# Blocks of 512 tokens in a two-stage feed-forward kernel, and the weights' signs moved by a rectifier

## The chip, the cores and the metric

The kernel runs on one core of one Trainium2 chip. The metric is the device time of one execution in microseconds (us). A kernel is timed several times and the median is given; one execution is also recorded by the hardware profiler, and its own time stands beside its span.

## The reference

The inputs are four batches of eight heads with 576 positions of 64 numbers. Two attentions are added: a global one over means of four positions, whose output is repeated four times, and a local one over the positions less than four apart. The sum, laid out as x with 2304 tokens by 512, goes through two feed-forward stages:

```
out_up   = repeat(softmax(scale * mean4(q) @ mean4(k).T) @ mean4(v), 4)
out_loc  = softmax(where(|i-j| < 4, scale * q @ k.T, -1e9)) @ v
x  = (out_up + out_loc) as [2304, 512]
h  = x @ w_in  ;  g = where(h > 0, h, exp(min(h, 0)) - 1)  ;  x2  = g @ w_out      # stage 1, w_in [512, 2048]
h2 = x2 @ w2_in ; g2 = s * max(h2, 0)**2 + b               ;  out = g2 @ w2_out    # stage 2
```

The weights arrive as 64-bit floats. The kernel makes 32-bit numbers of them on the chip, and splits these into a high and a low part, so that three products (high by high, low by high, high by low) replace one.

## The kernel before

The tokens are cut into nine blocks of 256 (N = 256, NSUB = 9), and the 2048 inner features into 16 slices of 128 (FC = 16). Work for a stage ph, a block j and a slice f is one unit: `ffn_h` makes h (12 matmuls of 256 columns, line 879), five elementwise instructions on ScalarE, VectorE and GpSimd turn it into gh and gl (lines 899 to 915 and the helpers at 303 to 311), and `ffn_x` adds g @ w_out to two accumulators. In stage 1 these are 12 matmuls of 256 columns (line 935), in stage 2 six of 512 columns (line 938), because there w_out is the moving operand.

The order of the units is a list. Blocks 0 and 1 of stage 1 are interleaved with an offset of five slices, blocks 2 to 6 follow one by one, blocks 7 and 8 (`LASTP` = 2) alternate slice by slice, and then stage 2 takes its nine blocks one by one. A slice of weights stays in one buffer for the whole of a stage; the slice of stage 2 takes the buffer when the last block of stage 1 has used it. Blocks 7 and 8 each have an x tile from a pool of two, which also served blocks 5 and 6.

Making one weight slice (`weights`, lines 340 to 370): two DMAs of 512 KB fill `raw`; ScalarE multiplies the upper words by 2^-112, which moves the exponent (line 303, raw<-raw); VectorE shifts the lower words right by 29 (line 357), puts the sign bit of the upper word into the lower (line 362), and adds the upper word shifted left by 3 (line 364); ScalarE copies the result to w's high part (line 303, w<-raw); GpSimd or VectorE subtracts for the low part (line 311). There are 16 slices in each stage.

Nothing of this has a fixed place. A planner (`Plan.emit`) keeps a list of operations with an assumed duration, a due time and the buffers that they take, and issues on each engine the operation that can start first, earlier due times going first. The due times come from the constants at the head of the file (T0 and P0 to P2 for the units, WL for the weights, A1 to DT for the attention). Where the planner sees TensorE idle, it puts matmuls on zeros (`keep_warm`, line 1139). So the record shows TensorE busy where it only waits, and line 1139 has to be read as idle time.

Of the kernel before, what the change touches and what calls it, by code (L numbers as in the profile page):

```python
# [21 lines left out]
DIRECT = 2  # L22
# [6 lines left out]
T0, P0, LB, TR, R0, P1, P2 = 39.86, 4.909, 5, 35.22, 2.175, 2.551, 2.783  # L29
VO, N0, N1, WL, RL, A1, A2, A3, AE, XL = 1.82, -7.55, 62.49, 11.29, -35.77, 25.65, -34.57, 3.08, 64.22, 29.58  # L30
DE, DS, DT = -1.26, 98.38, 75.88
LASTP, NREST, VP = 2, 4, -1.95
# [22 lines left out]
class Plan:  # L55
# [9 lines left out]
    WAIT = 1.607  # L65
# [162 lines left out]
def attn_moe_moe2(ctx, tc, q, k, v, w_in, w_out, w2_in, w2_out, s2, b2, mask, mask_d, out):  # L228
# [59 lines left out]
    x2d = [dram_buf(f"x2d{j}", [DM, N]) for j in range(NSUB)]  # L288
# [31 lines left out]
    order += [(0, j, f) for f in range(FC) for j in range(NSUB - LASTP, NSUB)]  # L320
    order += [(1, j, f) for j in range(NSUB) for f in range(FC)]
    due_at, t = {}, T0
    for ph, j, f in order:
        due_at[ph, j, f] = t
        t += P0 if ph == 0 and j < 2 else P1 if ph == 0 else P2

    def vt(ph, j, f):
        return due_at[ph, j, f]
# [4 lines left out]
    def weights(ph, f):  # L333
# [9 lines left out]
        for i in range(2):  # L343
            def ld(i=i):
# [10 lines left out]
        copy(lambda: high().bitcast(F32), lambda: high().bitcast(F32), 2 * DM, ("act",), scale=2.0 ** -112,  # L355
             r=rawp, w=[u], u=[raw], due=due)
# [10 lines left out]
        op("dve", 0.14 + 4 * DM / 960, cv, r=[u, shifted], w=[raw], due=due, lock=True)  # L367
# [9 lines left out]

    def x_buf(ph, j):
        if (ph, j) not in x_b:
            x = Buf(*((p1, "nat") if (ph, j) == (1, 0) else (p2, "x")), [128, 2, CC, N], F32R)  # L380
            x.part = [(Buf(None, "xhi", None), Buf(None, "xlo", None)) for _ in range(CC)]
            x_b[ph, j] = x
        return x_b[ph, j]
# [353 lines left out]
    def split(xb, c, o, m, src, r, due):  # L737
        xh, xl = (list(p) for p in zip(*(xb.part[c] if isinstance(c, slice) else [xb.part[c]])))
        n = m * (c.stop - c.start if isinstance(c, slice) else 1)
        copy(lambda: xb()[:, 0, c, o:o + m], src, n, r=r, w=xh, u=[xb], due=due)  # L740
        tt(lambda: xb()[:, 1, c, o:o + m], src, lambda: xb()[:, 0, c, o:o + m].bitcast(F32), ALU.subtract, n,
           r=r + xh, w=xl, u=[xb], due=due)
# [124 lines left out]
    def ffn_h(ph, j, f, n=N):  # L867
        due = vt(ph, j, f)
        third = ph == 0 and 2 <= j < NSUB - LASTP and 3 <= f < FC - 3 and f % 3 == 0
# [6 lines left out]
        def mm(run, first, last):  # L876
            def pe():
                for i, (wpart, xpart, c) in enumerate(run):
                    nc.tensor.matmul(ps(), lhsT=w()[:, wpart, 0, c * 128:(c + 1) * 128], rhs=x()[:, xpart, c, :],  # L879
# [11 lines left out]
        for i, (run, need) in enumerate(runs):  # L891
            op("pe", us * len(run), mm(run, i == 0, i == len(runs) - 1), r=need + [ps], w=[ps], u=[w, x], due=due, ffn=True)
        e = Buf(p2, "r", [128, n])
        gh, gl = Buf(p4, "gh", [128, n], F32R), Buf(p4, "gl", [128, n], F32R)
# [3 lines left out]
        if ph == 0:  # L898
# [6 lines left out]
            copy(gh, e, n, r=[r3], w=[gh], u=[e], due=due)  # L905
            tt(gl, e, lambda: gh().bitcast(F32), ALU.subtract, n, r=[r3, gh], w=[gl], u=[e], due=due)
        else:
# [5 lines left out]
               r=[r2], w=[gh], u=[e], due=due)  # L913
            op("dve", td + 0.07, lambda: nc.vector.scalar_tensor_tensor(  # L914
                out=gl(), in0=e(), scalar=sb2[:, 1:2], in1=gh().bitcast(F32), op0=ALU.add, op1=ALU.subtract),
               r=[r2, gh], w=[gl], u=[e], due=due, lock=True)
        return gh, gl

    def ffn_x(ph, j, f, g):
        gh, gl = g  # L920
        w = w_b[ph, f]
        due = vt(ph, j, f) + 3 * (P1 if ph == 0 else P2)
        if f == 0:
            acc_b[ph, j] = [Buf(ps_a, "acc", [128, 512]) for _ in range(2)]
        for a in range(2):
            acc = acc_b[ph, j][a]

            def pe(acc=acc, a=a):
                for i, (wpart, g) in enumerate(((0, gh), (1, gh), (0, gl))):
                    wo = w()[:, wpart, 1]  # L930
                    last = f == FC - 1 and i == 2
                    if ph == 0:
                        for c in range(2):
                            cc = 2 * a + c
                            nc.tensor.matmul(acc()[:, c * N:(c + 1) * N], lhsT=wo[:, cc * 128:(cc + 1) * 128], rhs=g(),  # L935
                                             start=(f == 0 and i == 0 and c == 0), stop=last and c == 1)
                    else:
                        nc.tensor.matmul(acc(), lhsT=g()[:, a * 128:(a + 1) * 128], rhs=wo,  # L938
                                         start=(f == 0 and i == 0), stop=last)

            op("pe", 0.712, pe, r=[w.out, gh, gl, acc], w=[acc], u=[w], due=due, ffn=True)
            if f == FC - 1:
                o = Buf(p2, "ev", [128, 512])
                if ph == 0:
                    copy(o, acc, 512, r=[acc], w=[o], due=due - 4)
# [3 lines left out]
                    continue  # L949
                parts = 2 if j == NSUB - 1 else 1  # L950
                n = 512 // parts
                for i in range(parts):
                    half, c = Buf(None, "half", None), slice(i * n, (i + 1) * n)
                    copy(lambda o=o, c=c: o()[:, c], lambda acc=acc, c=c: acc()[:, c], n, ("act", "dve")[i:] if parts > 1 else ("act", "dve"),
                         r=[acc], w=[half], u=[o], due=due - 4)
                    load(Buf(None, "out", None), 262144 // parts, lambda a=a, o=o, c=c: nc.sync.dma_start(
# [247 lines left out]
```

## Time and profile before

| | us |
|---|---|
| median of three runs (lowest, highest) | 979.16 (978.72, 982.04) |
| the profiled execution: its time, its span | 976.13, 974.0 |
| TensorE busy, of the span | 955.4, 98% |
| VectorE busy | 612.4, 63% |
| ScalarE busy | 473.0, 49% |
| GpSimd busy | 409.2, 42% |
| TensorE's granted clock in the 40 slices | 0.9 or more of full speed in each |

The engines are named PE (TensorE), PEld (its weight loads), DVE (VectorE), ACT (ScalarE), POOL (GpSimd) and SP (SyncE). A duration of a single matmul in the trace is about 284 ns for 256 columns, but matmuls overlap; what one costs is read from how far apart runs of them begin. Stage 1's last two blocks begin at about 466 us, stage 2 at about 566 us.

### The profile page before, as it was taken

Reading aid. Unit: us, or ns where it says so; the run is one execution under the profiler, and the core shown is the slowest. Engines: PE = TensorE matmul, PEld = TensorE weight load, DVE = VectorE, ACT = ScalarE, POOL = GpSimd, SP = SyncE. Lnnn points to the kernel's source line nnn. Section 1 sums busy time; section 2 is a strip of 40 time slices with the busy share of each in tenths; the row PEclk is TensorE's granted clock in tenths of the full one; section 3 lists DMA queues with packets and bytes.
Section 4 is the critical chain, followed back from the end, with each engine's and each line's share of the span. In section 5 each row is a group of like instructions: output and inputs, shape, how many; then the busy total and the mean of one; then the engine's idle time right before and its main releaser. Section 6 shows DMA issues by size and latency. Waiting matters only on the chain.

```text
span 974.0 us, 21374 instructions
## 1 busy us (share of the span) xinstructions
PE 955.4 (98%) x8420; PEld 892.2 (92%) x8420; DVE 612.4 (63%) x1058; ACT 473.0 (49%) x1239; POOL 409.2 (42%) x385
## 2 busy tenths in 40 slices
PE   8999999999999999999999999999999999999998
PEld 7888898999999999999999999999999999999997
DVE  5689888897787988887367797333334343333332
ACT  6687666555554455444665565333333333333332
POOL 5565556678776887775564543010101010010000
PEclk9999999999999999999999999999999999999999
DMA  9755656553433542443333451000101010100000
GB/s 198 200 141 175 192 162 155 136 161 83 127 99 99 123 110 64 100 115 109 109 131 130 152 183 57 23 28 17 44 1 45 1 44 1 44 2 22 1 23 22
DMA packets 102468, 88.34 MB, mean 91 GB/s; under 512 B 48864, under 2 KB 91872, under 8 KB 102368
## 3 DMA queue, kind: packets, MB, share of 16 engines
q1 hardware_dynamic: 100576, 86.54, 31.7%
q8 instruction: 66, 1.08, 0.5%
q10 hardware_dynamic: 1792, 0.44, 0.2%
q14 instruction: 34, 0.28, 0.1%
HBM read 73.85 MB, written 13.11 MB: 89 GB/s over the span
## 4 chain that ended last, share of the span: by engine, by line
PE 69%; DVE 11%; POOL 6%; issue 6%; DMA 4%; ACT 3%; SPq 1%; POOLq 0%; DVEq 0%; ACTq 0%
PE h L879 31%; PE acc L938 21%; PE acc L935 12%; POOL gl L311 2%; PE acc L879 2%; DVE raw L362 2%; DMA raw<-in_moe_w_out_dram 2%; DVE raw L364 2%; POOL w L311 1%; POOL wu L311 1%; DVE raw L357 1%; DVE w L311 1%; DVE raw L822 1%; DVE r L903 1%; DMA w<-in_k_dram 1%
## 5 line engine op out<-in xcount | busy, mean ns | idle before, releaser
L879 PE MATMUL h<-x,w 128*128 128x256 f32 x3024 | 407.0, 284 | 4.0 <-DVE r L903 2.9
L879 PEld LDWEIGHTS h<-x,w 128*128 128x128 f32 x3024 | 387.0, 188 | 19.1 <-DVE r L903 5.0
L935 PE MATMUL acc<-gh,w 128*128 128x256 f32 x1152 | 188.8, 285 | 0.0
L938 PE MATMUL acc<-w,gh 128*128 128x512 f32 x576 | 181.4, 396 | 0.0
L935 PEld LDWEIGHTS acc<-gh,w 128*128 128x128 f32 x1152 | 157.3, 189 | 2.6 <-issue 1.9
L311 POOL TENSOR_TENSOR x<-xr,x 128x256 fp32r<-128x256 f32 (+2 forms) x47 | 40.9, 892 | 262.5 <-DVE x L305 254.6
L909 DVE SCALAR_TENSOR_TENSOR r<-r,sb,h 128x256 f32<-128x256 f32 x144 | 68.9, 478 | 129.2 <-ACT r L908 129.2
L311 POOL TENSOR_TENSOR gl<-r,gh 128x256 fp32r<-128x256 f32 x127 | 111.7, 884 | 81.8 <-ACT gh L303 77.0
L914 DVE SCALAR_TENSOR_TENSOR gl<-r,sb,gh 128x256 fp32r<-128x256 f32 x144 | 77.8, 541 | 101.8 <-ACT gh L912 101.8
L912 ACT ACTIVATE gh<-r,sb 128x256 fp32r<-128x256 f32 x144 | 73.2, 508 | 101.3 <-PE acc L938 86.2
L908 ACT ACTIVATE r<-h 128x256 f32<-128x256 f32 x144 | 55.0, 382 | 130.2 <-PE h L879 129.8
L935 PE MATMUL acc<-gl,w 128*128 128x256 f32 x576 | 115.6, 282 | 0.0
L938 PE MATMUL acc<-w,gl 128*128 128x512 f32 x288 | 113.5, 394 | 0.0
L938 PEld LDWEIGHTS acc<-w,gh 128*128 128x128 f32 x576 | 99.3, 188 | 13.7
L311 POOL TENSOR_TENSOR w<-raw,w 128x512 fp32r<-128x512 f32 x48 | 66.5, 1397 | 60.3 <-ACT w L303 55.8
L935 PEld LDWEIGHTS acc<-gl,w 128*128 128x128 f32 x576 | 88.6, 188 | 0.0
L903 DVE SCALAR_TENSOR_TENSOR r<-r,h 128x256 f32<-128x256 f32 x124 | 50.7, 414 | 54.3 <-ACT r L901 49.3
L303 ACT ACTIVATE gh<-r 128x256 fp32r<-128x256 f32 x144 | 58.3, 413 | 50.4 <-DVE r L903 27.6
L899 ACT ACTIVATE r<-h 128x256 f32<-128x256 f32 x124 | 46.8, 378 | 66.3 <-PE h L879 39.0
L938 PEld LDWEIGHTS acc<-w,gl 128*128 128x128 f32 x288 | 54.1, 188 | 13.5 <-DVE gl L914 0.3
L822 DVE TENSOR_REDUCE raw<-wu 128x128 f32<-128x896 f32 x36 | 63.6, 1787 | 2.0 <-POOL wu L311 1.9
L901 ACT ACTIVATE r<-r 128x256 f32<-128x256 f32 x144 | 60.0, 417 | 3.9
(144 smaller groups left out, 1170.4 us busy)
## 6 DMA issues: line engine op xcount, KB each, us to landing
raw<-in_moe_w_in_dram SPq DMA_DIRECT2D x32, 512.0 KB
raw<-in_moe_w_out_dram SPq DMA_DIRECT2D x32, 512.0 KB
raw<-in_k_dram SPq DMA_DIRECT2D x17, 320.0 KB
raw<-in_v_dram SPq DMA_DIRECT2D x17, 320.0 KB
x2d<-ev SPq DMA_DIRECT2D x18, 256.0 KB
xr<-x2d SPq DMA_DIRECT2D x18, 256.0 KB
out_dram<-ev SPq DMA_DIRECT2D x16, 256.0 KB
vg<-in_v_dram SPq DMA_DIRECT2D x12, 288.0 KB
```

The lines of the kernel that those rows point to most:

```text
L303: a = (0.11 + n / 1200, lambda: nc.scalar.activation(out=out(), in_=src(), func=ACTF.Copy, scale=scale))
L311: f = lambda e: lambda: e.tensor_tensor(out=out(), in0=in0(), in1=in1(), op=alu)
L822: op("dve", 0.07 + 14 * D / 546, lambda: nc.vector.tensor_reduce(out=vo()[:, WD + j * D:WD + (j + 2) * D].rearrange("p (j d) -> p j d", j= ...
L879: nc.tensor.matmul(ps(), lhsT=w()[:, wpart, 0, c * 128:(c + 1) * 128], rhs=x()[:, xpart, c, :], start=first and i == 0, stop=last and i == ...
L901: op("act", ta, lambda: nc.scalar.activation(out=e(), in_=e(), func=ACTF.Exp, scale=-1.0), r=[r1], w=[r2], u=[e], due=due)
L903: op("dve", td, lambda: nc.vector.scalar_tensor_tensor(out=e(), in0=e(), scalar=-1.0, in1=ps(), op0=ALU.add, op1=ALU.max), r=[r2, ps], w=[ ...
L908: op("act", ta, lambda: nc.scalar.activation(out=e(), in_=ps(), func=ACTF.Relu), r=[ps], w=[r1], u=[e], due=due)
L909: op("dve", td + 0.07, lambda: nc.vector.scalar_tensor_tensor(out=e(), in0=e(), scalar=sb2[:, 0:1], in1=ps(), op0=ALU.mult, op1=ALU.mult), ...
L912: op("act", ta + 0.1, lambda: nc.scalar.activation(out=gh(), in_=e(), func=ACTF.Identity, bias=sb2[:, 1:2]), r=[r2], w=[gh], u=[e], due=due)
L914: op("dve", td + 0.07, lambda: nc.vector.scalar_tensor_tensor(out=gl(), in0=e(), scalar=sb2[:, 1:2], in1=gh().bitcast(F32), op0=ALU.add, o ...
L935: nc.tensor.matmul(acc()[:, c * N:(c + 1) * N], lhsT=wo[:, cc * 128:(cc + 1) * 128], rhs=g(), start=(f == 0 and i == 0 and c == 0), stop=l ...
L938: nc.tensor.matmul(acc(), lhsT=g()[:, a * 128:(a + 1) * 128], rhs=wo, start=(f == 0 and i == 0), stop=last)
```

## The change

Three things are changed, and the planner's constants with them.

Blocks 7 and 8 of stage 1 become one block of 512 tokens, and stage 2's blocks 1 to 8 become four such blocks; stage 2's block 0 stays at 256. A wide unit has 12 matmuls of 512 columns for h, and 12 of 512 columns into four accumulators: two of their usual pool, two of the pool that the attention's transposes used. At the last slice the accumulators come in the order 2, 3, 0, 1. The x of a wide block has its high and its low part in two tiles of their own: the high one in the pool "x", the low one in "nat" (or "raw", for stage 2's blocks 3 and 7). The gh and gl of a wide unit share a tile that goes round three buffers of the attention (T, vw, vg). `ffn_x` follows two units behind `ffn_h` in wide blocks, three in the others.

The ScalarE copy with the factor 2^-112 becomes a Prelu with the same factor and a slope of -2^32 for negative numbers. A negative word becomes positive with an exponent 32 higher, and the later shift by 3 carries this bit into the sign's place. The VectorE instruction of line 362 is gone.

```diff
-T0, P0, LB, TR, R0, P1, P2 = 39.86, 4.909, 5, 35.22, 2.175, 2.551, 2.783
+T0, P0, LB, TR, R0, P1, P2 = 36.7, 5.112, 5, 34.78, 2.153, 2.551, 2.603
...
-    order += [(0, j, f) for f in range(FC) for j in range(NSUB - LASTP, NSUB)]
-    order += [(1, j, f) for j in range(NSUB) for f in range(FC)]
+    order += [(0, NSUB - 2, f) for f in range(FC)]
+    order += [(1, j, f) for j in (0, *range(1, NSUB, 2)) for f in range(FC)]
+    wide = {(0, NSUB - 2), *((1, j) for j in range(1, NSUB, 2))}
...
-        copy(lambda: high().bitcast(F32), lambda: high().bitcast(F32), 2 * DM, ("act",), scale=2.0 ** -112,
-             r=rawp, w=[u], u=[raw], due=due)
+        op("act", 0.11 + 2 * DM / 1200, lambda: nc.scalar.activation(
+            out=high().bitcast(F32), in_=high().bitcast(F32), func=ACTF.Prelu, scale=2.0 ** -112, alpha=-2.0 ** 32),
+            r=rawp, w=[u], u=[raw], due=due)
...
-            nc.vector.scalar_tensor_tensor(out=low(), in0=high(), scalar=-0x80000000, in1=low(),
-                                           op0=ALU.bitwise_and, op1=ALU.bitwise_or)
...
+    class X:
+        def __init__(self, ph, j):
+            if (ph, j) in wide:
+                lo = (p2, "raw") if ph and j % 4 == 3 else (p1, "nat")
+                self.tiles = [Buf(*t, [128, CC, 2 * N], F32R) for t in ((p2, "x"), lo)]
+                self.at = lambda i: self.tiles[i]()
...
-    def ffn_h(ph, j, f, n=N):
+    def ffn_h(ph, j, f):
         due = vt(ph, j, f)
+        n = 2 * N if (ph, j) in wide else N
...
+        else:
+            e = Buf(p2, "wu", [128, n])
+            both = Buf(p1, ("T", "vw", "vg")[len(wides) % 3], [128, 2, n], F32R)
+            gh, gl = Buf(None, "gh", None), Buf(None, "gl", None)
...
-        due = vt(ph, j, f) + 3 * (P1 if ph == 0 else P2)
+        two = (ph, j) in wide
+        due = vt(ph, j, f) + (4 if two else 3) * (P1 if ph == 0 else P2)
+        tiles = 4 if two else 2
         if f == 0:
-            acc_b[ph, j] = [Buf(ps_a, "acc", [128, 512]) for _ in range(2)]
-        for a in range(2):
+            acc_b[ph, j] = [Buf(*((ps_a, "acc") if a < 2 else (ps_t, "at")), [128, 512]) for a in range(tiles)]
+        last = f == FC - 1
+        for k, a in enumerate((2, 3, 0, 1) if two and last else range(tiles)):
...
+                    if ph == 0 and two:
+                        nc.tensor.matmul(acc(), lhsT=wo[:, a * 128:(a + 1) * 128], rhs=g(), start=first, stop=end)
...
-        drain(LAG + (ph == 0 and j < 2))
+        drain(2 if (ph, j) in wide else LAG + (ph == 0 and j < 2))
```

`load_x` loads the x of a wide block in two steps of 256 tokens, from the same kind of DMAs, and splits each step as before. The last block's evictions keep their form: the last two accumulators are evicted in halves by ScalarE and VectorE, the two before them whole.

## Rows read from the trace of the kernel before

**Rows 1.** Windows: length; PE, PEld, DVE, ACT, POOL busy; PEclk, DMA share, GB/s.
```profile
25.00:75.00 50.00, 47.25 (x834) 42.64 (x830) 37.90 (x75) 37.26 (x135) 27.55 (x28) 1.00 0.68 170
75.00:225.00 150.00, 144.84 (x1776) 135.61 (x1776) 132.57 (x229) 91.08 (x239) 95.64 (x93) 1.00 0.58 162
225.00:465.00 240.00, 238.11 (x2027) 232.59 (x2026) 197.09 (x316) 117.19 (x343) 179.07 (x147) 1.00 0.38 101
465.00:580.00 115.00, 113.06 (x925) 110.13 (x925) 79.03 (x96) 73.08 (x149) 67.31 (x60) 1.00 0.43 142
580.00:960.00 380.00, 380.00 (x2413) 343.95 (x2412) 149.70 (x297) 136.15 (x296) 26.66 (x31) 1.00 0.07 25
```

**Rows 2.** Windows, line 1139 (matmuls on zeros) alone: PE and PEld busy.
```profile
25.00:75.00 50.00, 17.99 (x279) 15.80 (x279) 1.00 0.68 170
75.00:225.00 150.00, 8.12 (x121) 6.96 (x121) 1.00 0.58 162
...
465.00:580.00 115.00, 2.24 (x37) 2.07 (x37) 1.00 0.43 142
```

**Rows 3.** Chain, 616 to 625 us: start, us, engine, tile, line, instructions merged.
```profile
617.94 1.44 PE h L879 x12
619.38 1.40 PE acc L938 x6
```

**Rows 4.** Chain, 380 to 640 us: long runs of one width.
```profile
596.71 5.62 PE acc L938 x24
602.33 5.73 PE h L879 x48
```

**Rows 5.** Chain, 295 to 325 us: a run in stage 1.
```profile
305.02 2.88 PE acc L935 x24
```

**Rows 6.** Timeline, 463 to 473 us: the last split of block 8's x, the wait.
```profile
465.98 1.31 POOL L311 TENSOR_TENSOR x<-xr,x 128x512 fp32r<-128x512 f32 x1 [3.27 <-ACT x L303]
...
468.94 2.24 PE L1139 MATMUL at<-wz 128*128 128x128 bf16 x37
```

**Rows 7.** Waits of PE, 465 to 580 us: total, times, longest.
```profile
PE h L879 <- DVE r L903: 1.8, 3, 0.8
```

**Rows 8.** Chain, 20 to 235 us: shares of this stretch by line.
```profile
by line: PE acc L935 12.1%; PE h L879 11.8%; DMA raw<-in_moe_w_out_dram 7.9%; issue 6.7%; DVE raw L362 6.3%; DVE raw L364 4.9%; DVE raw L357 3.7%; DVE w L311 3.7%; PE at L714 2.7%; POOL gl L311 2.7%; POOL p L311 2.4%; PE acc L1139 2.3%; DMA
```

**Rows 9.** Windows, line 362 alone: DVE busy.
```profile
25.00:175.00 150.00, 23.77 (x16) 1.00 0.62 169
440.00:610.00 170.00, 21.88 (x16) 1.00 0.38 124
```

**Rows 10.** Groups by line and shape: busy, mean ns, idle before by releaser.
```profile
L364 DVE SCALAR_TENSOR_TENSOR raw<-raw 128x1024 int32<-128x1024 int32 x32 | 45.1, 1410 | 1.1
L357 DVE TENSOR_SCALAR raw<-raw 128x1024 int32<-128x1024 int32 x32 | 34.9, 1090 | 2.5 <-DMA raw<-in_moe_w_out_dram 2.5
...
L857 DVE TENSOR_TENSOR xr<-at,T 128x512 f32<-128x512 f32 x4 | 2.7, 684 | 4.5 <-PE at L846 2.6 <-POOL x L311 1.9
...
L912 ACT ACTIVATE gh<-r,sb 128x256 fp32r<-128x256 f32 x144 | 73.2, 508 | 101.3 <-PE acc L938 86.2 <-DVE r L909 15.1
...
L303 ACT ACTIVATE gh<-r 128x256 fp32r<-128x256 f32 x144 | 58.3, 413 | 50.4 <-DVE r L903 27.6 <-PE acc L935 21.6 <-PE h L879 0.6
...
L303 ACT ACTIVATE raw<-raw 128x1024 f32<-128x1024 f32 x32 | 36.9, 1154 | 0.9 <-DMA raw<-in_moe_w_out_dram 0.8
L303 ACT ACTIVATE w<-raw 128x1024 fp32r<-128x1024 f32 x32 | 36.6, 1145 | 40.6 <-DVE raw L364 40.4
...
L303 ACT ACTIVATE x<-xr 128x512 fp32r<-128x512 f32 x9 | 5.7, 630 | 6.6 <-DVE xr L857 5.1 <-PE h L879 1.3
...
L1021 ACT ACT_TABLE_LOAD x1 | 1.3, 1283 | 2.9 <-issue 2.9
...
L311 POOL TENSOR_TENSOR w<-raw,w 128x512 fp32r<-128x512 f32 x48 | 66.5, 1397 | 60.3 <-ACT w L303 55.8 <-PE at L523 4.5
...
L311 POOL TENSOR_TENSOR x<-xr,x 128x512 fp32r<-128x512 f32 x9 | 12.6, 1398 | 7.6 <-ACT x L303 7.6
```

More of the change, by code (lines that the diff above doesn't have):

```diff
@@ L935, in pe @@
                             nc.tensor.matmul(acc()[:, c * N:(c + 1) * N], lhsT=wo[:, cc * 128:(cc + 1) * 128], rhs=g(),
-                                             start=(f == 0 and i == 0 and c == 0), stop=last and c == 1)
+                                             start=first and c == 0, stop=end and c == 1)
                     else:
[L938 to L945, printed above, removed]
+                        nc.tensor.matmul(acc(), lhsT=g()[:, a * 128:(a + 1) * 128], rhs=wo, start=first, stop=end)
+            op("pe", 0.70 if two or ph else 0.712, pe, r=[w.out, gh, gl, acc], w=[acc], u=[w] + gu, due=due, ffn=True)
+            if not last:
+                continue
+            final = ph == 1 and j == NSUB - 2
+            o = Buf(p2, "xr" if final and k < 2 else "ev", [128, 512])
+            if ph == 0:
+                copy(o, acc, 512, r=[acc], w=[o], due=due - 4)
+                if two:
+                    load(x2d[j], 262144, lambda a=a, o=o: nc.sync.dma_start(out=x2d[j].t[a * 128:(a + 1) * 128, :], in_=o()), due, r=[o])
+                else:
                     load(x2d[j], 262144, lambda a=a, o=o: nc.sync.dma_start(
@@ L948, in ffn_x @@
                         in_=o().rearrange("p (c t) -> p c t", c=2)), due, r=[o])
[L949 to L956, printed above, removed]
-                        out=out[j * N + a * 128:j * N + (a + 1) * 128, c], in_=o()[:, c]), due, r=[half], u=[o])
+                continue
+            parts = 2 if final and k >= 2 else 1
+            n = 512 // parts
+            for i in range(parts):
+                half, c = Buf(None, "half", None), slice(i * n, (i + 1) * n)
+                copy(lambda o=o, c=c: o()[:, c], lambda acc=acc, c=c: acc()[:, c], n, ("act", "dve")[i:] if parts > 1 else ("act", "dve"),
+                     r=[acc], w=[half], u=[o], due=due - 4)
+                load(Buf(None, "out", None), 262144 // parts, lambda a=a, o=o, c=c: nc.sync.dma_start(
+                    out=out[j * N + a * 128:j * N + (a + 1) * 128, c], in_=o()[:, c]), due, r=[half], u=[o])
     def load_x(ph, j):
@@ L984, in load_x, with ld @@
[L984 to L985 removed]
+        t0, t1 = j * N, (j + 1 + ((ph, j) in wide)) * N
+        end = t1 if ph else min(t1, max(t0, DIRECT * S))
+        for at in range(t0, end, N):
+            cols = []
+            t, e = at, min(at + N, end)
+            while t < e:
+                if ph:
+                    jj = min(t // N, NSUB - 2)
+                    src, o, m = x2d[jj], t - jj * N, N
+                else:
+                    jj, o = divmod(t, HS)
+                    src, m = xd[divmod(jj, 2)], min(e - t, HS - o)
+                cols.append((src, o, m))
+                t += m
+            n, o = e - at, at - t0
+            for c2 in range(2):
+                t = Buf(p2, "xr", [128, 2, N])
+                def ld(t=t, c2=c2, cols=cols):
+                    done = 0
+                    for src, o, m in cols:
+                        nc.sync.dma_start(out=t()[:, :, done:done + m],
+                                          in_=src.t[c2 * 256:(c2 + 1) * 256, o:o + m].rearrange("(c p) t -> p c t", p=128))
+                        done += m
+                load(t, 1024 * n, ld, due - 12, r=[c[0] for c in cols], n=len(cols))
+                for c in range(2):
+                    split(xb, 2 * c2 + c, o, n, lambda t=t, c=c, n=n: t()[:, c, :n], [t], due - XL)
@@ L988, in attn_moe_moe2 @@
+        for o in range(max(end, t0) - t0, t1 - t0, 128) if ph == 0 else ():
+            load_direct(xb, o, [divmod((t0 + o) // 64 + g, NT64) for g in range(2)], due)
     units = [Unit(b, hp) for b in range(B) for hp in range(HP)]
```

83 lines of the change are left out of this document (35 added, 48 removed).

## The prediction

> **What bounds the kernel now.** I read the page first: TensorE is busy 98% of the span. That share hides waits, because line 1139 fills them, so I went to the windows, and to line 1139 alone in the same windows [rows 1, 2]. The reader is to see three stretches.
>
> From 580 us on TensorE is busy 380.00 of 380 us with no fill and the other engines far below (VectorE 149.70). Here only the cost of TensorE's own work counts.
>
> From 225 to 580 us it is nearly so: 238.11 of 240, and 113.06 of 115 less 2.24 of fill.
>
> From 25 to 225 us TensorE stands still or turns over zeros for 50 - 47.25 + 17.99 = 20.7 us and 150 - 144.84 + 8.12 = 13.3 us, 34 us in all. VectorE is busy 132.57 of 150 there. So I took the chain of this stretch [rows 8]: three of the weights' VectorE steps stand on it, line 362 with 6.3% of 215 us = 13.5 us. The sixteen executions of line 362 there take 23.77 us [rows 9]; a bit over half of their time is on the chain.
>
> The granted clock is 1.00 in every window [rows 1], the level of 2.4 GHz, before and, since TensorE stays as busy, after.
>
> **Part 1: columns.** In stage 2 a run of 12 matmuls of 256 columns begins 1.44 us before the next run, 120 ns each; a run of six of 512 takes 1.40 us, 233.3 ns each [rows 3]. Stage 1 has the first price too: 2.88 us for 24 [rows 5]. So a wide matmul costs 2 x 120.0 - 233.3 = 6.7 ns less than the two that it replaces. The wide ones that replace pairs are 12 of h per slice in stage 2, 4 blocks x 16 slices x 12 = 768 (its line 938 has 512 columns already), and 24 per slice in stage 1's last block, 16 x 24 = 384. The sum is 1152 x 6.7 ns = 7.7 us, all on the path.
>
> The trace has no h of 512 columns with x as the moving operand. From long runs of one width, 5.73 us / 48 = 119.4 ns and 5.62 / 24 = 234.2 ns [rows 4], the gain is 4.6 ns a pair, 5.3 us. The upper bound is the clock's: 512 columns at the granted 2.4 GHz are 213.3 ns, 26.7 ns a pair, 30.7 us; no run of 512 in these rows comes near it. I take 7.7, from the steady rows.
>
> The Trainium skill, "TensorE: Matmul & The Clock Gate", section "Back-to-back issue gap", gives an isolated gap of N/2.4 + 2.5 ns, in which only the 2.5 ns is saved by a wider matmul: by it the sum would be an estimated 2.9 us. The trace differs: it shows 120.0 ns where the page gives 109.2, and 233.3 where it gives 215.8, so I go by the rows.
>
> **Part 2: the beginning of the wide block of stage 1.** Blocks 7 and 8 start together at 466 us, and block 8's x comes last: its split on GpSimd runs from 465.98 to 467.29, and TensorE turns over zeros for 2.24 us from 468.94 [rows 6]. Block 8's x tile was block 6's neighbour in a pool of two, so it could be written only as block 6 ended. In the wide block the high part takes the slot that block 5 has left, and the low part "nat", which the attention has given up by then: x can be ready before block 6 ends. I take the 2.2 us as gained; bounds 0 (the attention of batch 3 is what comes last) and 2.2 plus the 1.8 us of part 3.
>
> **Part 3: h's accumulators.** TensorE's waits in 465 to 580 us are for line 903, 1.8 us in three [rows 7]: with two h buffers, h waits until VectorE has read the one before last. In the wide block the same two buffers cover two units of 5.6 us instead of two of 2.88. I take 1.5 of the 1.8 us; bounds 0 and 1.8.
>
> **Part 4: line 362 gone.** In the last block and in stage 2's block 0 the sixteen cost 21.88 us of VectorE [rows 9], but TensorE hardly waits there, so they are worth nothing beyond part 3. In the front the most that they can give is their share of the chain, 13.5 us, and the least nothing: DMA of the weights has 7.9% of the same chain, 17 us [rows 8], and a slice that isn't held by VectorE may be held by its data. I take half, 6.7 us, since VectorE is busy 88% of 75 to 225 us, the DMA share is 0.58 [rows 1], and the 34 us of idle and fill leave room. What comes late next are the DMA, lines 364 and 357 (1410 and 1090 ns a slice [rows 10]), and further on the attention of batches 2 and 3: in 225 to 465 us VectorE has 197.09 of 240 us and GpSimd 179.07, so blocks 2 to 6 can move 7 us earlier without either being full.
>
> **Edits costed at nothing.** Prelu for Copy: 1154 ns before, the nearest plain copy 1145 [rows 10], so 0; with a further operand as in line 912 it would be 508 - 413 = 95 ns more, 32 x 95 = 3.0 us on an engine that is busy 61% of 75 to 225 us and less than that on the path. Two accumulators from the transposes' pool: at each end of a wide block they must be evicted before the next block's first `ffn_x`; accumulators 0 and 1 (1.4 us) and an h of 2.8 us lie between, against two evictions of about 0.63 us as for x<-xr; without that cover it is 1.3 us at each of four ends, 5 us. The shared gh and gl tile: three in turn, where two units are pending. x's low part in "raw": it waits for the weights' last slice; block 3's x is due two blocks after that. The DMAs (x2, x, output) keep their number and size on SP's queue, but for block 0's neighbours. The tail is the same four halves. The new planner constants reorder everything a little; I give this 3 us to either side and no sign.
>
> **Sum.** 7.7 + 2.2 + 1.5 + 6.7 = 18.1 us. The profiled execution took 976.13 us and would take 958.0. That execution was 3.0 us under the median of 979.16; the median becomes 961.1 us.
>
> **The rivals.**
>
> *The front doesn't move.* The data or the attention of batch 1 hold the slices as long as VectorE did. For it: the DMA's 7.9% of the chain, and due times for blocks 0 and 1 that are further apart (P0 5.112 for 4.909). Against it: VectorE's 88%. Then only parts 1 to 3 count, 11.4 us: 967.8 us. Chance 0.22.
>
> *The whole chain share comes off.* For it: fill at line 1139 of 26.1 us in the front [rows 2]. Against it: a chain seldom loses a link without another taking part of its place. 11.4 + 13.5 = 24.9 us: 954.3 us. Chance 0.13.
>
> *The gains are eaten up.* Wide matmuls at the long runs' price (5.3 us), the front unmoved, x of the wide block still late, and 3 us lost by the new order: 979.2 - 5.3 + 3 = 976.9 us. Chance 0.08.
>
> *Slower: the wide chain outlasts its cover.* Place: stage 1's wide block, while stage 2's weights are made. For one unit the chain from h to gl is Relu, Exp and the copy at 0.63 each, line 903 at 0.68 (as line 857, of 512 elements) and GpSimd at 1.40, 4.0 us [rows 10]. The cover from the end of h to its own `ffn_x` is two h and one `ffn_x`, 3 x 2.8 = 8.4 us. With a whole slice of weights queued ahead on every engine (ScalarE 2.30, VectorE 2.50, GpSimd 2.79, 7.6 us) the chain is 11.6 us and TensorE waits 3.2 us in each of 16 units, 51 us at worst. It decides from 18.1 / 16 = 1.1 us a unit; at half the worst, 25.5 us, the time is 961.1 + 25.5 = 986.6 us. Against it: the chain of 256-token units in the same stretch cost TensorE 1.8 us in all [rows 7], the planner puts the units' steps first, and line 362 is gone there. Chance 0.04.
>
> *Slower: Prelu needs another table.* One table load of 1283 ns stands in the whole trace [rows 10], though Exp, Relu, Copy and Identity alternate. If Prelu were in another set, every slice would need two more loads, 2.57 us on ScalarE; 9 of 16 slices on the front's chain make 23 us lost against part 4's 6.7: 979.2 - 11.4 - 6.7 + 23 = 984 us. Against it: four functions share one load, and a plain rectifier is among them. Chance 0.03. The Trainium skill, "ScalarE: Activation LUTs", section "Table sets: the hidden batching unit", says that cheap functions are in every set, which would exclude this rival, but its list does not name Prelu; its price for a switch, 2.66 us, would make the 23 us an estimated 48 us. No row here shows a switch in mid-run.
>
> **How the numbers follow.** The forecast, 961.1 us, has 0.50; its own range, from part 4's neighbours and the 3 us of reordering, is 955 to 967. The other cases have 0.22, 0.13, 0.08, 0.04 and 0.03. The range of 950 to 974 takes in the first three cases with their spread and leaves the last three out, and some of the edges. A measurement of this kernel tells about 0.5% (4.9 us) from no change: faster means under 974.3, slower over 984.1. The first three cases are faster but for a little of their spread, and of the eaten gains a small part: 0.85. Within 0.5%: 0.09. Slower: 0.06.
>
> **What would show it.** Step 1: in stage 2 runs of line 879 and 938 at 233 ns a matmul, and a wide block of 89.6 us. If the h of 512 columns costs 240 ns, part 1 is gone. Step 2: no fill between blocks 6 and 7. Step 3: no wait for line 903 after 465 us. Step 4: line 1139 in 25 to 225 us at some 20 us instead of 26, and block 7 of stage 1 beginning near 460 us on the profile's axis instead of 466. A second table load would prove the last rival, waits of h or acc behind gl in the wide block of stage 1 the one before it. I am wrong if stage 2 takes as long as before, or if the wide block begins no earlier.

## The result, and the profile after

The changed kernel took 951.6 us in the median of four executions (949.7 to 953.9). The kernel before took 980.6, its three times from above and a fourth. The ratio is 0.971, 95% interval 0.967 to 0.975; of 979 us that is 28.4 us. Timed again later, beside other runs of the kernel before, the ratio was 0.973 (0.970 to 0.975), 26.6 us. The profiled execution took 953.3 us with a span of 951.5, against 976.13 and 974.0. The forecast of 961.1 us had the sign, and 18.1 us of the gain; the time lies at the fast edge of the range (950 to 974), 2.7 us from the rival in which the whole chain share of line 362 comes off (954.3). Of all executions below one, of the run e5, took 1812.4 us, for no reason that is known, and it is left out of that run's time and ratio.

The page's first part, after (share of the span, number of instructions):

```profile
PE 939.4 (99%) x7096; PEld 826.2 (87%) x7096; DVE 522.2 (55%) x868; ACT 438.9 (46%) x1068; POOL 414.0 (44%) x378
```

VectorE lost 90 us of work. Of this line 362 was 45.6 us [rows 9]; most of the rest lies in the elementwise instructions of the wide blocks, which are half as many and each less than twice as long.

The windows after, columns as in [rows 1], and then the fill alone (line 1178 is line 1139 of before), as in [rows 2]:

```profile
25.00:75.00 50.00, 47.13 (x751) 42.66 (x748) 27.37 (x69) 37.52 (x135) 29.80 (x32) 0.90 0.60 162
75.00:225.00 150.00, 148.41 (x1784) 140.09 (x1783) 113.71 (x219) 93.20 (x247) 107.98 (x103) 1.00 0.63 169
225.00:452.00 227.00, 226.33 (x1938) 220.53 (x1938) 194.59 (x308) 111.39 (x327) 173.70 (x140) 1.00 0.39 104
452.00:545.00 93.00, 93.00 (x429) 76.19 (x428) 47.28 (x51) 58.91 (x87) 55.97 (x41) 1.00 0.41 136
545.00:940.00 395.00, 395.00 (x1772) 322.00 (x1771) 124.04 (x177) 120.39 (x197) 33.60 (x36) 1.00 0.09 31
```

```profile
25.00:75.00 50.00, 13.38 (x176) 10.78 (x176) 0.90 0.60 162
75.00:225.00 150.00, 4.88 (x69) 3.94 (x69) 1.00 0.63 169
...
452.00:545.00 93.00, 0.00 (x0) 0.00 (x0) 1.00 0.41 136
```

The reader is to see three things. From 452 us on TensorE has no idle time and no fill left. Between 75 and 225 us idle time and fill fell from 13.3 us to 150 - 148.41 + 4.88 = 6.5 us, and between 25 and 75 us from 20.7 to 16.3 us; VectorE went from 132.57 us in the longer of the two to 113.71. And the clock is 0.90 between 25 and 75 us, where it was 1.00.

The chain of 20 to 235 us after, to be held against [rows 8]:

```profile
by line: PE h L894 23.9%; PE acc L964 22.1%; PE at L726 4.9%; DMA vg<-in_v_dram 3.7%; PE acc L1178 3.6%; issue 3.2%; PE acc L894 2.8%; PE h L726 2.6%; DVE raw L364 2.0%; PE at L535 2.0%; DMA nat<-in_q_dram 1.8%; PE at L1178 1.6%; DVE raw L8
```

The weights' VectorE steps, 14.9% before in three entries, are down to line 364 with 2.0% among those shown; TensorE's own work took their place, and DMA of the attention's inputs (vg, nat) is the next releaser. The DMA of the weights, 7.9% before, is not among the largest any more.

**Where the 22.5 us of the two profiled executions lie.** Block 5 of stage 1 is evicted 7.4 us earlier, with 1200 h matmuls begun in both; from the timeline of ScalarE, before and after:

```profile
418.89 1.07 ACT L303 ACTIVATE ev<-acc 128x512 f32<-128x512 f32 x2
```

```profile
411.54 0.60 ACT L303 ACTIVATE ev<-acc 128x512 f32<-128x512 f32 x1 [0.88 <-PE acc L964]
```

Stage 1's last matmuls end at 565.5 us before and at 548.35 after, 17.2 us earlier, from the chain of each:

```profile
564.08 1.43 PE acc L935 x12
565.51 1.43 PE h L879 x12
```

```profile
546.95 1.40 PE acc L960 x6
548.35 4.31 PE h L894 x36
```

In both, 36 of stage 2's h matmuls had been done by then. The last matmul begins at 969.55 and 947.03 us, so stage 2 gave 5.4 us, the blocks 6 to 8 of stage 1 gave 9.8, and what lies before them 7.4. This last number is held down by the clock, which the changed kernel's profiled execution lost for a while:

```profile
26.00:32.00 6.00, 3.64 (x60) 3.37 (x60) 3.44 (x8) 3.12 (x13) 2.12 (x4) 1.00 1.11 229
32.00:44.00 12.00, 11.91 (x136) 10.98 (x137) 4.75 (x8) 6.81 (x15) 5.87 (x6) 0.57 0.62 164
```

TensorE is busy 3.64 of 6 us, and in the 12 us that follow the granted clock is 0.57 in the mean, 12 x 0.43 = 5.2 us of full clock lost. Executions of this kernel at a clock of 1.00 took 949.7 and 949.9 us, so the loss cost some 3.5 us of the 953.3.

The prediction's sign for the front was fill of some 20 us in 25 to 225 us and a begin near 460 us. The fill is 13.38 + 4.88 = 18.3 us. The wide block's first matmul begins at 452.98 us. The 466 us of before is where blocks 7 and 8 begin to alternate; block 7's first h stood at 458.30, and block 6 was finished behind it. So the begin moved by 5 us by that mark and by 13 by the other, and the eviction above, 7.4 us, is the better measure.

### The profile page after: what moved, and what is told of

Same layout as the page of the kernel before. It is cut to its first block, busy times and chain, and to the rows that moved or that the text cites. A ratio compares the mean times of both kernels' runs of the same rounds, so it can differ in the third digit from the quotient of the medians.

```text
span 951.5 us, 18034 instructions
## 1 busy us (share of the span) xinstructions
PE 939.4 (99%) x7096; PEld 826.2 (87%) x7096; DVE 522.2 (55%) x868; ACT 438.9 (46%) x1068; POOL 414.0 (44%) x378
## 4 chain that ended last, share of the span: by engine, by line
PE 88%; DVE 4%; ACT 2%; issue 2%; DMA 2%; POOL 2%; SPq 0%; DVEq 0%; POOLq 0%; ACTq 0%
PE h L894 37%; PE acc L964 14%; PE acc L967 12%; PE at L967 9%; PE acc L894 2%; PE at L960 2%; PE acc L960 2%; PE at L726 1%; PE at L1178 1%; DMA nat<-in_q_dram 1%; DVE raw L834 1%; DMA vg<-in_v_dram 1%; PE acc L1178 1%; PE at L627 1%; PE h L726 1%
## 5 line engine op out<-in xcount | busy, mean ns | idle before, releaser
L894 PE MATMUL h<-x,w 128*128 128x256 f32 (+1 forms) x1936 | 342.4, 323 | 1.4 <-DVE r L927 0.6
L894 PEld LDWEIGHTS h<-x,w 128*128 128x128 f32 x1936 | 285.1, 189 | 34.5 <-DVE r L927 1.3
L964 PE MATMUL acc<-gh,w 128*128 128x256 f32 x896 | 147.7, 286 | 0.0
L933 DVE SCALAR_TENSOR_TENSOR wu<-wu,sb,h 128x512 f32<-128x512 f32 x64 | 47.8, 747 | 128.5 <-ACT wu L932 128.5
L932 ACT ACTIVATE wu<-h 128x512 f32<-128x512 f32 x64 | 38.3, 598 | 127.2 <-PE h L894 126.8
L311 POOL TENSOR_TENSOR wu<-raw 128x896 f32<-128x896 f32 x28 | 59.8, 2147 | 9.1 <-DVE raw L834 7.8
L923 ACT ACTIVATE r<-h 128x256 f32<-128x256 f32 x92 | 34.8, 378 | 59.8 <-PE h L894 32.1
L894 PE MATMUL h<-nat,w 128*128 128x512 f32 x192 | 52.4, 394 | 0.0
L364 DVE SCALAR_TENSOR_TENSOR raw<-raw 128x1024 int32<-128x1024 int32 x32 | 46.7, 1460 | 9.3 <-ACT raw L356 8.0
L303 ACT ACTIVATE w<-raw 128x1024 fp32r<-128x1024 f32 x32 | 36.4, 1138 | 10.7 <-DVE raw L364 10.4
```

Source lines behind the costliest of these rows:

```text
L303: a = (0.11 + n / 1200, lambda: nc.scalar.activation(out=out(), in_=src(), func=ACTF.Copy, scale=scale))
L311: f = lambda e: lambda: e.tensor_tensor(out=out(), in0=in0(), in1=in1(), op=alu)
L932: op("act", ta, lambda: nc.scalar.activation(out=e(), in_=ps(), func=ACTF.Relu), r=[ps], w=[r1], u=[e], due=due)
```

## The experiments

The experiments were timed in five rounds beside the kernel before, in three batches, with three to twelve executions each; the ratio is to the kernel before of the same batch. Its medians were 979.3 us (e1 to e4), 976.6 (e5 to e9) and 977.5 (the last four), so across batches ratios are to be compared, not medians. The last column is the ratio's distance from 1, times 979 us.

| kernel | median us | ratio, 95% interval | us |
|---|---|---|---|
| the change | 951.6 | 0.971 (0.967 to 0.975) | -28.4 |
| the change again, with the last four | 951.0 | 0.973 (0.970 to 0.975) | -26.6 |
| e1: Prelu alone, old constants | 967.7 | 0.988 (0.984 to 0.991) | -11.9 |
| e5: Prelu alone, new constants | 963.2 | 0.986 (0.984 to 0.987) | -13.9 |
| e7: wide alone, old constants | 971.4 | 0.9955 (0.994 to 0.997) | -4.4 |
| e4: wide and Prelu, old constants | 956.9 | 0.978 (0.974 to 0.981) | -21.8 |
| e2: wide, new constants, no Prelu | 980.5 | 1.002 (0.9995 to 1.004) | +1.9 |
| e3: the change, stage 2 narrow | 955.8 | 0.976 (0.972 to 0.980) | -23.8 |
| e8: the change, VectorE busier | 980.3 | 1.004 (1.003 to 1.006) | +4.1 |
| e11: the same with a reduction | 960.1 | 0.982 (0.980 to 0.985) | -17.4 |
| e9: the change, longer chain | 960.0 | 0.984 (0.983 to 0.986) | -15.3 |
| e10: the change, still less VectorE | 953.1 | 0.975 (0.972 to 0.977) | -25.0 |
| e12: the change, longer fill | 950.8 | 0.972 (0.970 to 0.975) | -27.2 |

**e1, the Prelu alone** in the kernel before:

```diff
-        copy(lambda: high().bitcast(F32), lambda: high().bitcast(F32), 2 * DM, ("act",), scale=2.0 ** -112, ...
+        op("act", ..., lambda: nc.scalar.activation(..., func=ACTF.Prelu, scale=2.0 ** -112, alpha=-2.0 ** 32), ...
...
-            nc.vector.scalar_tensor_tensor(out=low(), in0=high(), scalar=-0x80000000, in1=low(), ...
...
-        op("dve", 0.14 + 4 * DM / 960, cv, r=[u, shifted], w=[raw], due=due, lock=True)
+        op("dve", 0.07 + 2 * DM / 960, cv, r=[u, shifted], w=[raw], due=due, lock=True)
```

The last two lines tell the planner that the step is shorter, so the order shifts with it.

> The kernel before with the Prelu in place of the copy and of line 362, nothing else changed (order and planner constants of before). In the changed kernel the 512-token block of stage 1 begins at 453 us where block 7 began at 466, 13 us earlier, twice what the prediction gave to line 362. Theory A (line 362 alone moved the front): block 7 begins 9 to 13 us earlier here, the time is 968 to 973 us against 980.6. Theory B (the planner's constants and the new order moved it): block 7 begins 0 to 4 us earlier, 976 to 981 us. Stage 2 takes as long as before in both.

Measured 967.7 us, by the ratio 11.9 less: theory A, a little under its 968 to 973. This is part 4 by itself, nearly twice the 6.7 us that it was given, and within the bound of 13.5. The position that theory A named came out smaller: blocks 7 and 8 begin to alternate at 459.10 us instead of 466.03, 6.9 us earlier and not 9 to 13. The profiled execution was the slowest of six (969.6 us), and its granted clock was 0.80 from 32 to 57 us, 25 x 0.20 = 5.0 us of full clock. In its chain of 20 to 235 us no VectorE line of the weights is among the twelve largest; the largest releaser outside TensorE there is the DMA of the weights, 6.4%.

**e2, the changed kernel without the Prelu** (the same edit backwards).

> The changed kernel with the sign moved by line 362 on VectorE again, as before; wide blocks and constants of the change. Theory A: the 512-token block begins at 462 to 466 us again, the time is 961 to 965 us against the changed kernel's 951.6. Theory B: it begins at 453 to 456, 952 to 956 us. VectorE's steps don't touch stage 2 after its first block, so from the start of the wide block on both lose at most 2 us.

980.5 us: dearer than either theory. All that the change gives is gone with line 362 alone. So neither theory is the whole: with line 362 the constants of the change cost something (this run against e7 below, which has the old ones), and without it they are worth something (e4). Most of the cost shows in 75 to 190 us, all engines and the fill alone, of this run and then of e7:

```profile
75.00:190.00 115.00, 110.62 (x1422) 103.09 (x1422) 89.81 (x166) 72.67 (x189) 68.36 (x62) 0.99 0.57 157
75.00:190.00 115.00, 9.93 (x130) 8.31 (x130) 0.99 0.57 157
```

```profile
75.00:190.00 115.00, 110.42 (x1351) 103.34 (x1350) 100.01 (x175) 74.52 (x191) 69.73 (x68) 1.00 0.56 162
75.00:190.00 115.00, 1.63 (x20) 1.19 (x20) 1.00 0.56 162
```

Idle and fill make 4.38 + 9.93 = 14.3 us here and 4.58 + 1.63 = 6.2 us there. VectorE is less busy here (89.81 us for 100.01), so what costs is not VectorE's load by itself but, it seems, the order.

**e3, stage 2 narrow** (the last block's evictions take the form of the kernel before with it):

```diff
-    order += [(1, j, f) for j in (0, *range(1, NSUB, 2)) for f in range(FC)]
-    wide = {(0, NSUB - 2), *((1, j) for j in range(1, NSUB, 2))}
+    order += [(1, j, f) for j in range(NSUB) for f in range(FC)]
+    wide = {(0, NSUB - 2)}
...
```

> The changed kernel with stage 2 in nine blocks of 256 tokens; the wide block of stage 1 and the Prelu stay. By the columns alone (768 wide matmuls at 233.3 ns for 1536 at 120.0) it is 5.1 us slower than the changed kernel, 956.7 us, and two neighbouring blocks of 256 take 90.8 us where a wide one takes 89.5. Rival: the gain of stage 2 lies at the borders of its blocks or in the shared tiles; then two blocks take 89.5 us here too.

955.8 us, 2.8 to 4.6 more than the changed kernel by the two ratios of that. The evictions, in the timeline, of two neighbouring narrow blocks here, and of two wide ones of the changed kernel:

```profile
684.48 1.29 ACT L303 ACTIVATE ev<-acc 128x512 f32<-128x512 f32 x2 [0.43 <-PE acc L967]
729.91 1.29 ACT L303 ACTIVATE ev<-acc 128x512 f32<-128x512 f32 x2 [0.43 <-PE acc L967]
```

```profile
682.46 1.30 ACT L303 ACTIVATE ev<-at 128x512 f32<-128x512 f32 x2
771.96 1.30 ACT L303 ACTIVATE ev<-at 128x512 f32<-128x512 f32 x2
```

A narrow block takes 45.43 us, two take 90.86, a wide one 89.50 (forecast: 89.6). Four times the difference is 5.4 us, what stage 2 gave above: the price of columns is what stage 2 gained, and no border adds to it.

**e4, the changed kernel with the constants of before** (four lines at the head of the file, of which the diff above shows the first, and WAIT in the planner).

> The changed kernel with the planner constants of the kernel before. Theory A: only the order shifts, 949 to 956 us. Theory B: the gain of the front, up to 13 us, goes with the constants, 958 to 965 us, and the 512-token block begins near 462 to 466 us.

956.9 us, just outside what theory A allows (949 to 956): the constants are worth some 5 us (0.978 against 0.971 and 0.973), and the order is not neutral. Over half of it shows in front of the wide block, where TensorE turns over zeros until x is there:

```profile
457.28 1.74 PE L1178 MATMUL at<-wz 128*128 128x128 bf16 x28
458.85 0.61 PE L858 MATMUL at<-ident,xr 128*128 128x128 f32 x4
459.30 1.61 PE L1178 MATMUL at<-wz 128*128 128x128 bf16 x26
```

These 3.35 us are more than the 2.24 of before [rows 6], which part 2 took to be gone with the wide block.

**e5, Prelu and new constants on narrow blocks** (e1 with the five lines of the change).

> The kernel before (blocks of 256 throughout) with the Prelu and with the planner constants of the change. With the constants of before the Prelu alone gave 967.7 us, and putting line 362 back into the changed kernel cost 28.9 us, far more than the 11.6 us that the Prelu won there. Theory A (the constants suit a kernel whose weight slices need less of VectorE, whatever the blocks): 5 us faster than 967.7, as for the changed kernel (956.9 to 951.6), so 961 to 965 us. Rival (the constants suit the wide blocks): 967 to 972 us.

963.2 us, in theory A's range. By the ratios the constants gave 2 us here, by the medians 4.5; the intervals of 0.988 and 0.986 overlap, but the three executions (960.9 to 963.8) all lie under the six of e1 (965.7 to 969.6), which ran on another chip. That the constants suit the lean weights rather than the wide blocks is likely, since e2 shows them to be of no use to wide blocks with line 362; it is not shown by the time alone.

**e7, wide blocks with line 362 and the old constants.**

> The changed kernel's wide blocks with line 362 on VectorE and with the constants of before: columns and blocks alone. The prediction's parts 1 to 3 are 11.4 us: 968 us. Rival: with line 362 the wide block of stage 1 and the weights of stage 2 get into each other's way, as the 980.5 us of the wide blocks without the Prelu suggests, and the gain is under 5 us: 975 to 979 us.

971.4 us, and by the ratio 4.4 us gained: the rival, which allowed under 5, though its 975 to 979 us were reckoned from a slower batch. The profile says where the rest went. The window of stage 2's first block, all engines and the fill alone:

```profile
545.00:615.00 70.00, 68.64 (x433) 59.37 (x432) 56.73 (x69) 39.50 (x72) 37.52 (x29) 1.00 0.42 141
545.00:615.00 70.00, 3.87 (x63) 3.52 (x63) 1.00 0.42 141
```

TensorE idles and fills for 1.36 + 3.87 = 5.2 us there. The changed kernel does not (70.00 of 70 us, no fill), and neither does e4, which differs from this run by the Prelu alone. In the chain of this run, here cut at 604 us, the last piece of it stands between the last slices:

```profile
596.24 2.80 PE acc L968 x12
599.03 2.98 PE at L1179 x53
602.01 2.06 PE h L895 x14
```

Stage 1 ended about 6 us earlier than before (559.3 us for 565.5), and the sixteen slices for stage 2 came no earlier: ScalarE's last copy to a w ends at 601.0 us, before at 600.8, in e4 at 583.0. So line 362 was not free in that stretch: it was free only as long as stage 1 ended late. Another 2.8 us of fill stand in front of the wide block, much as in e4.

**e8 and e11, VectorE busier; e9, the chain longer.** e8 adds an instruction beside the chain, whose result the low part overwrites; e11 puts a reduction in its place; e9 applies the factor in two ScalarE instructions.

```diff
+        op("dve", 0.07 + 2 * DM / 960, lambda: nc.vector.scalar_tensor_tensor(
+            out=w()[:, 1], in0=src(), scalar=1.0, in1=src(), op0=ALU.mult, op1=ALU.subtract),
+            r=[raw], w=[extra], u=[raw, w], due=due, lock=True)                                  # e8
...
+        op("dve", 0.07 + 2 * DM / 960, lambda: nc.vector.tensor_reduce(
+            out=w()[:, 1, :, 0:1], in_=src()[:, :, None, :], axis=AX.X, op=ALU.max),
+            r=[raw], w=[extra], u=[raw, w], due=due)                                             # e11
...
+        copy(..., 2 * DM, ("act",), scale=2.0 ** -56, r=rawp, w=[half], u=[raw], due=due)        # e9, then Prelu with 2^-56
```

> The changed kernel with one more VectorE instruction of 1024 elements for each weight slice, as long as line 362 but beside the chain: it runs while ScalarE makes the slice's high part, and its result is overwritten. Theory A (VectorE's time is what line 362 cost): 965 to 980 us. Theory B (its place in the slice's chain is what it cost): 951 to 957 us.

> The run with one more VectorE instruction beside the chain (980.3 us) once more, but with a reduction of 1024 elements to one for each half in its place, one operand in and almost nothing out, about 1.2 us. If it is VectorE's time that counts: four fifths of the 28.7 us, 970 to 980 us. If what counts is that a two-operand instruction shuts GpSimd out: 951 to 957 us.

> The changed kernel with the factor 2^-112 applied in two ScalarE instructions of 1.15 us, a copy and a Prelu with 2^-56 each: the slice's chain is 1.15 us longer and VectorE as free as before. Theory A (VectorE's time): 951 to 957 us. Theory B (the chain's length): 962 to 975 us, four fifths of what line 362 costs.

e8: 980.3 us, the whole gain back, as in e2 (28.7 us by the medians, 30.7 to 32.5 by the ratios). e9: 960.0 us, between the theories, 8 to 9 us up by the medians and 11 to 13 by the ratios. By these two VectorE's time would be the larger part of what line 362 cost, and the chain's length, or ScalarE's time, not nothing.

e11 does not bear that out: 960.1 us, only 9 us more, between its two theories and in the range of neither. Its reductions take nearly as long as e8's instructions. The groups of VectorE in 25 to 225 us, of e8 and then of e11:

```profile
L371 DVE SCALAR_TENSOR_TENSOR w<-raw 128x1024 fp32r<-128x1024 f32 x16 | 21.1, 1318 | 0.1
L359 DVE TENSOR_SCALAR raw<-raw 128x1024 int32<-128x1024 int32 x16 | 20.8, 1302 | 1.3 <-DMA raw<-in_moe_w_out_dram 1.2
```

```profile
L371 DVE TENSOR_REDUCE w<-raw 128x2 fp32r<-128x1024 f32 x16 | 19.4, 1210 | 0.1
L359 DVE TENSOR_SCALAR raw<-raw 128x1024 int32<-128x1024 int32 x16 | 14.1, 884 | 2.0 <-DMA raw<-in_moe_w_out_dram 2.0
```

In e8 the shift of line 359 became slower too, 1302 ns for 884. Most of the 20 us between the two runs lie at one place, the beginning of block 2, which needs the attention of batch 1: fill in 190 to 230 us, of e8, of e11 and of the changed kernel:

```profile
190.00:230.00 40.00, 18.34 (x257) 17.12 (x257) 0.91 0.50 132
```

```profile
190.00:230.00 40.00, 4.03 (x60) 3.48 (x60) 1.00 0.52 141
```

```profile
190.00:230.00 40.00, 3.25 (x49) 2.81 (x49) 1.00 0.44 121
```

Before, it was 6.49 us there. In e8's chain of 190 to 225 us this is the fill's share, and a VectorE multiplication of the attention that took 4.28 us stands before it:

```profile
192.65 4.28 DVE wu L311
199.04 5.25 PE acc L1182 x54
208.42 4.18 PE acc L1182 x73
216.28 3.12 PE acc L1182 x54
```

The timeline has it beside GpSimd's instructions:

```profile
192.36 0.73 POOL L520 TENSOR_TENSOR nat<-nat 72x256 f32<-72x256 f32 x1
192.57 4.36 DVE L311 TENSOR_TENSOR wu<-raw,ds 128x896 f32<-128x896 f32 x1
193.05 1.29 POOL L311 TENSOR_TENSOR s<-s,grs 72x288 f32<-72x288 f32 x2
194.30 1.69 POOL L311 TENSOR_TENSOR wu<-raw,ds 128x896 f32<-128x896 f32 x1
```

GpSimd is busy from 192.36 to 195.99 us without a break, and the multiplication ends 0.94 us later; the shortest of its kind in this run took 1.09 us. The added instructions differ in the same way. Their shortest, median and longest, of e8 and then of e11:

```profile
L371 DVE SCALAR_TENSOR_TENSOR w<-raw x32: 1200/1226/2214, 30.4 to 607.8; 128x1024 fp32r<-128x1024 f32 x32
L371 DVE TENSOR_REDUCE w<-raw x32: 1176/1216/1224, 31.8 to 586.5; 128x2 fp32r<-128x1024 f32 x32
```

Of e8's 32, the 18 that ran while an instruction of GpSimd ran took 1539 ns in the mean, the other 14 took 1221; e11's sixteen and sixteen took 1213 and 1216. So the price of a VectorE instruction in the front is not its length: e8's kind is held up beside GpSimd, and the reduction is not. GpSimd is held up in its turn: its five gl instructions that ran beside one of e8's took 1187 ns in the mean, five alone 735, and the seven beside one of e11's 740. The 318 ns in 18 of e8's make 5.7 us and not 20. How much of the rest comes from these hold-ups, and how much from the planner's order (it takes the one instruction, and not the other, as excluding GpSimd), these runs don't tell; nor whether it is the second operand or the larger output that makes the difference.

Of e11's 9 us 3.19 are fill in front of the wide block (420 to 470 us), as in e4.

**e10, without the shift**, with the last step a shift alone (this kernel leaves out the three lowest bits of each weight):

```diff
-        op("dve", 0.07 + DM / 960, lambda: nc.vector.tensor_scalar(out=low(), in0=low(), scalar1=29, ...
-            nc.vector.scalar_tensor_tensor(out=low(), in0=high(), scalar=3, in1=low(), ...
+            nc.vector.tensor_scalar(out=low(), in0=high(), scalar1=3, scalar2=None, op0=ALU.logical_shift_left)
```

> The changed kernel without line 359 (the shift of the lower words, 0.83 us a slice) and with line 364 as a shift alone; this leaves out the three lowest bits of each weight. VectorE has some 1.4 us less for each slice (0.83 and the difference of a shift alone to 1.46), as much as line 362 had. If VectorE's time still bounds the front (theory A): 935 to 945 us. If the DMA or the attention are next, as the prediction put it: 947 to 953 us, as the changed kernel.

953.1 us, as the changed kernel: less work for VectorE gave nothing more. VectorE is busy 71.08 us of 75 to 190 us there, and 86.86 in the changed kernel; TensorE 113.50 and 113.41 of 115. After line 362 VectorE's work on the weights no longer bounds the front.

**e12, fill in longer matmuls, and the changed kernel again:**

```diff
-        for _ in range(int(us / (128 / (1200.0 if cold else 2400.0) + 0.003))):
-            nc.tensor.matmul(o, lhsT=wz, rhs=wz, start=True, stop=True)
+        for m in (512, 128):
+            ...
+                nc.tensor.matmul(o[:, :m], lhsT=wz, rhs=wz[:, None, :].to_broadcast([128, m // 128, 128]), ...
```

> The changed kernel with the fill of line 1178 made of matmuls of 512 columns (and a rest of 128) instead of 128: a quarter of the instructions for the same time. In the profile of the changed kernel TensorE stood for 2.36 us at 28.5 us behind 40 short fills, and the granted clock was at its lower level from 33.2 to 43.5 us. If the stand comes of the many instructions, it goes, the clock holds in the front, and the time is 947 to 950 us in each execution; if not, 950 to 954 us as the changed kernel.

> The changed kernel as it is, on the same chip as the three others: 949 to 954 us.

950.8 and 951.0 us, no difference; clocks of 0.990 to 0.998 in the one and 0.989 to 0.998 in the other. The stand of 2.36 us was not in the second profile of the changed kernel either, and yet the granted clock was 0.66 there from 26 to 31 and again from 36 to 41 us. So the stand came in one of two profiles, and the falls of the clock don't hang on it. No version here beats the changed kernel.

## Why the prediction was right, and where it was not

**Part 1, columns, 7.7 us: right.** Stage 2 gave 5.4 us of the profiled pair (its share of the forecast was 768 x 6.7 ns = 5.1), a wide block 89.50 us. The changed kernel's chain has the run that was missing before, h of 512 columns with x as the moving operand:

```profile
673.33 1.40 PE acc L967 x6
674.73 1.40 PE at L967 x6
676.13 2.80 PE h L894 x12
```

2.80 / 12 = 233 ns, as the product with w_out. The rule of the Trainium skill ("TensorE: Matmul & The Clock Gate", "Back-to-back issue gap") would have made it 2.5 ns a pair, an estimated 1.9 us in stage 2; the row's 6.7 ns held. Stage 1's share, 384 x 6.7 ns = 2.6 us, was not measured by itself.

**Part 3, 1.5 us: right. Part 2, 2.2 us: the size was right, the reason was not.** Idle time and fill of TensorE in two windows, in us; the first holds the begin of block 7 or of the wide block (in e2 that lies in the second):

| kernel | 420 to 470 | 470 to 545 |
|---|---|---|
| before | 1.09 + 1.46 | 1.19 + 1.18 |
| e1: Prelu, narrow, old constants | 0.76 + 1.57 | 2.48 + 0 |
| e5: Prelu, narrow, new constants | 0.06 + 0 | 2.24 + 0 |
| e7: line 362, wide, old constants | 0.57 + 3.36 | 0 + 0.56 |
| e4: Prelu, wide, old constants | 0.61 + 3.35 | 0 + 0 |
| e2: line 362, wide, new constants | 0 + 1.12 | 0 + 2.63 |
| the change: Prelu, wide, new constants | 0.05 + 0 | 0 + 0 |

The second column is part 3: each wide block takes the idle time away (before, waits for h's accumulators), and no narrow one does. The first column is part 2, and there the width takes nothing away. The slots in "x" and "nat" did not bring x in time by themselves, in e4 and e7; the fill is gone where the new constants and the Prelu come together, in narrow blocks as well. What x waited for in e4 is open. Of the 9.8 us that blocks 6 to 8 gave in the profiled pair the two windows make 4.9 and the columns, by the row, 2.6; the rest is not accounted for.

With the columns the two parts made 11.4 us in the forecast; wide blocks gave 21.8 - 11.9 = 9.9 us on top of the Prelu (e1, e4), and 4.4 without it (e7).

**Part 4, line 362: the mis-sized term.** Forecast 6.7 us, "half" of its chain share of 13.5; measured 11.9 (8.4 to 15.5 by e1's interval). The half was a compromise between two bounds. The row nearest to it was VectorE's 88% between 75 and 225 us, which spoke for the upper one. And the sentence that the second sixteen "are worth nothing beyond part 3" holds for narrow blocks (e1 has stage 2 as long as before) and failed for wide ones: there they cost the 5.2 us of e7. By the ratios the Prelu is worth 21.8 - 4.4 = 17.4 us in the wide kernel with old constants, near 11.9 + 5.2; with intervals of 3 to 4 us to either side, so close an agreement is luck. What made line 362 dear, VectorE's time, its place in the chain or its hold-ups with GpSimd, the runs e8, e9 and e11 leave open.

**The constants, 0 with 3 us to either side: too little.** They give 4.8 to 6.6 us with the Prelu and wide blocks (e4, by the two ratios of the change), and cost 1.9 + 4.4 = 6.3 us without the Prelu (e7, e2). The terms are 11.9 + 9.9 + 4.8 to 6.6 us, against the forecast's 6.7 + 11.4 + 0. That they sum to the measured 26.6 to 28.4 proves nothing, as each is a difference of two of these ratios; in another order of the edits the shares differ.

**The clock.** The prediction kept 1.00 before and after, "since TensorE stays as busy". In the changed kernel's profile it was 0.90 from 25 to 75 us, some 3.5 us of that execution's time, which the forecast did not have.

**The rivals.** The front did move. The whole chain share came off, nearly: that rival, given 0.13, has the nearest time, 954.3 us. That nearness is partly luck, since its sum has nothing for the constants: with the old ones the kernel took 956.9 us (e4). By the same token the range held only by 1.6 us, and the forecast's 18.1 us are about two thirds of the gain. The wide chain did not outlast its cover. Prelu needed no other table: the changed kernel has one table load, and Prelu costs what the copy cost. The Trainium skill, "ScalarE: Activation LUTs", section "Table sets: the hidden batching unit", says that cheap functions are in every set; that Prelu behaves as one of them is what this trace adds. The two groups of ScalarE's view of the changed kernel:

```profile
L356 ACT ACTIVATE raw<-raw 128x1024 f32<-128x1024 f32 x32 | 36.6, 1145 | 1.9 <-DMA raw<-in_moe_w_out_dram 1.9
L1060 ACT ACT_TABLE_LOAD x1 | 1.3, 1283 | 2.9 <-issue 2.9
```

**What was named as next** (the DMA of the weights, lines 364 and 357) fits e1, where that DMA is the largest releaser outside TensorE. In the changed kernel it is the DMA of the attention's inputs, which the prediction did not name. e10 shows only that it is not VectorE's work on the weights.

## What to carry to other kernels

An operation that looks free because its engine's consumer arrives late is free only until something upstream gets faster: two edits, each with a price of its own, were worth 4.4 and 11.9 us alone and 21.8 together. Where one engine is near 90% busy in a stretch and its steps stand on the chain there, a removed step can give most of its chain share, here 11.9 of 13.5 us, and not half; and look for the point, as in e10, from which more of the same gives nothing. Cross the edits with each other before you say which of them removed a wait: here the constants and the Prelu removed the one that had been put down to the wide block. Wider matmuls gave their fixed part, here 6.7 ns a pair of 256 columns, times their number.

## What the runs showed of the hardware

The clock goes with the spread. The kernel before took 975.0 to 987.5 us in seventeen executions of one batch; the span was 972.9 us at a mean granted clock of 0.999 and 985.4 at 0.987, 12.5 us for the 0.012 x 974 = 11.7 us of full clock that were missing. It is not always the whole of what is missing: the changed kernel took 949.7 us at 1.00 and 953.9 at 0.992, 4.2 us for 0.008 x 948 = 7.6. In the changed kernel's first profile the fall to the lower level (1.2 GHz; 0.50 of full speed from 35 to 40 us) came behind a stand of TensorE of 2.36 us in the front, where the work comes in short pieces; in its second profile falls came without such a stand. So two profiled executions can differ by several microseconds from the two medians (22.8 us against 29.0 here): compare clocks first.

VectorE and GpSimd held each other up, and not with every instruction: beside GpSimd the two-operand instruction of e8 took 1539 ns in the mean for 1221 alone, the shift of line 359 in the same run 1383 for 688, but the reduction of e11 1213 for 1216.
